# Sharing vector work by a port, placing small transposes, and unsplit products for eight more tiles in a fused attention and feed-forward kernel

## The chip, the cores and the metric

The kernel runs on one NeuronCore of one Trainium2 chip. The metric is device time of one execution in microseconds (us), as a median of several. The engines are named as in the profile: PE (TensorE, the matrix engine; PEld is its loading of the stationary operand), DVE (VectorE), ACT (ScalarE), POOL (GpSimd) and SP (SyncE, which here issues nearly all DMAs).

## The reference

Local attention with a few global tokens, followed by a maxout feed-forward layer over all 4352 tokens. Shortened:

```
# 8 batches, 8 heads, 512 local and 32 global tokens, head dimension 64, all float32
s_g  = scale * q_g @ [k_g, k_l]^T ; out_g = softmax(s_g) @ [v_g, v_l]
s_l  = scale * [q_l @ k_g^T, mask(q_l @ k_l^T, |i - j| <= 32)]
out_l = softmax(s_l) @ [v_g, v_l]
x = concat(out_g, out_l) laid out as (4352 tokens, 512)
h = max(max(x @ w1, x @ w2), x @ w3)          # w1, w2, w3: 512 x 768
out = h @ w_out                               # 768 x 512
```

The weights come in as 64-bit numbers and are made into float32 in the kernel.

## The kernel before, in words

**Tiles.** A tile is 128 query rows of two heads: 128 tiles in all, four (t = 0 to 3) for each pair of heads p, sixteen for each batch. The order is SEQ: tiles 0, 1, 4, 5, ... of the first batch, then in number order from 16 on. `i` counts places in SEQ; from 16 on, i and the tile's number are the same.

**Products.** [...] A split product writes a number as a float32r high part plus a float32r rest and adds two or three products; it needs vector work to make the parts (`copy` makes the high part, line 99; `sub` the rest, line 92). An unsplit product takes the float32 numbers as they are. Scores of tiles in NATK (0 to 19 before) and products with the values of tiles below NAT (20 before) are unsplit; for the others `split_q`, `split_k`, `split_v` and the second halves of `trans`, `transg` and `pv` do the splitting. The feed-forward layer is split throughout.

**One pass of the loop (line 548) for tile i.** `trans(i+1)` puts four transposes of the next tile's probabilities on PE (lines 345 and 346, into the one PSUM tile T) and moves them out; `scores(i+3)` (line 297) makes scores on PE, masks and takes the minimum of the negated scores on DVE (L325), exponentiates on ACT (L327), scales by the inverse sum with `times` (L111, L113 or L115, whichever engine gets it), and a DMA on SP's queue then writes them as float32r into `prob`; `pv(i)` (line 374) multiplies the transposed probabilities with the values. Once for each four tiles, `glob` and `glob_soft` do the same for the global queries, and `glob_soft` issues six DMAs into `probg`. `transg` (line 357) transposes one 128x128 piece of `probg` (L364) and puts its columns into the same tile `pt` that `pv` reads. In the kernel before, `transg` of tile i+1 stands late in pass i, three feed-forward products after `pv(i)`.

**Feed-forward work as filling.** `fill(n)` puts n feed-forward products (L424 layer one, L445 layer two) on PE between these steps: 21 a pass for i < 32, 18 after. Batch 0 is done from i = 8 on with 256-wide products in layer one, the others 512 wide. The weights (24 pieces) are turned into float32 by `convert` (lines 154 to 172) in the passes up to i = 23: four operations on DVE over SBUF data (L161, L162, L165, L166), a `copy` and a `sub` for each piece.

**Who does the vector work.** `least` (line 82) holds a planned load for DVE, ACT and POOL and gives each `copy`, `sub` and `times` to the engine with the lowest planned load after it; the costs are formulas in the width n. `settle(4500)` (line 87) keeps an engine that was idle from being far behind in the plan.

```
load = {"a": 0.0, "d": 0.0, "p": 0.0}
e = min(costs, key=lambda e: load[e] + costs[e]); load[e] += costs[e]
```

The tile framework places the recorded instructions of the engines and adds the waits; each engine then runs its own list in order, and so does each DMA queue.

Of the kernel before, what the change touches and what calls it, by code (L numbers as in the profile page):

```python
# [20 lines left out]
NP = H // 2  # L21
# [1 line left out]
KW = 576  # L23
NEG = -8.0e9

NATK = range(0, 20)
HIMAX = float(np.array(0x47EFFFFF, np.int32).view(np.float32))


# [25 lines left out]
def body(ctx, tc, kin, qin, vin, min_, win, out):  # L55
# [12 lines left out]
    small = ctx.enter_context(tc.tile_pool(name="small", bufs=2))  # L68


    load = {"a": 0.0, "d": 0.0, "p": 0.0}

    def width(ap):
        n = 1
        for x in ap.shape[1:]:
            n *= x
        return n

    def spend(e, ns):
        load[e] += ns  # L80

    def least(costs):
        e = min(costs, key=lambda e: load[e] + costs[e])
        load[e] += costs[e]
        return e

    def settle(ns):
        top = max(load.values()) - ns
        for e in load:
            load[e] = max(load[e], top)  # L90

    def sub(out, a, b, psum=False):
        n = width(out)
        c = {"d": n * 1.04 + (160 if psum else 110)}
        if not psum:
            c["p"] = n * 2.32 + 130
        (dve if least(c) == "d" else pool).tensor_tensor(out=out, in0=a, in1=b, op=ALU.subtract)  # L97

    def copy(out, a, psum=False):
        n = width(out)  # L100
        c = {"d": n * (1.04 if psum else 0.52) + (160 if psum else 150), "a": n * 0.833 + (150 if psum else 190)}
        if least(c) == "d":
            dve.tensor_copy(out=out, in_=a)
        else:
            act.copy(out=out, in_=a)  # L105

    def times(out, a, col):
        n = width(out)
        e = least({"d": n * 0.52 + 125, "a": n * 0.833 + 185, "p": n * 1.27 + 150})
        if e == "d":  # L110
            dve.tensor_scalar(out=out, in0=a, scalar1=col, scalar2=None, op0=ALU.mult)  # L111
        elif e == "a":
            act.activation(out=out, in_=a, func=AF.Copy, scale=col)  # L113
        else:
            pool.tensor_scalar(out=out, in0=a, scalar1=col, scalar2=1.0, op0=ALU.mult, op1=ALU.mult)  # L115
# [38 lines left out]
    def convert(n):  # L154
        r = raw[n].bitcast(I32).rearrange("p (n t) -> p n t", t=2)
        if n < 18:
            c = spare[n // 2 % 2 if n < 15 else 1][:, n % 2]
# [6 lines left out]
        yield  # L164
        dve.scalar_tensor_tensor(out=c, in0=r[:, :, 1], scalar=-0x40000000, in1=c, op0=ALU.bitwise_and, op1=ALU.bitwise_or)  # L165
        dve.scalar_tensor_tensor(out=c, in0=r[:, :, 0], scalar=29, in1=c, op0=ALU.logical_shift_right, op1=ALU.bitwise_or)  # L166
        spend("d", 1900)
        yield
        wt[n] = const.tile([128, 1024], F32R, name=f"w{n}", tag=f"w{n}")
        copy(weight(n, 0), f32(c))  # L170
# [18 lines left out]


    NS = 4 * B * NP
    NAT = 20
    EARLY = 16
    SEQ = [4 * p + t for h in range(2) for p in range(NP) for t in (2 * h, 2 * h + 1)] + list(range(16, NS))
    kraw, kst, qraw, qs, vraw, vs, xr, sc, pg, pts = [{} for _ in range(10)]
# [320 lines left out]
    def tile_at(i):  # L516
        return SEQ[i] if i < NS else NS
# [30 lines left out]
    for i, sl in enumerate(SEQ):  # L548
        p, t = divmod(sl, 4)
        b = p // NP  # L550
        settle(4500)
        if i % 16 == 0 and b > 1:
            fill(400)
            mm[0] = moe_local(b - 1)
        trans(tile_at(i + 1))
        first = i < 32
        fill(6 if first else 4)
        next_scores(i + 3)
        if i < 16:
            if i == 7:  # L560
                clear()
            if i in (10, 12):
                load_k((i - 2) // 2)
            if i == 14:
                split_k(5)
                load_k(6)
        elif t == 3:
            split_k(p + 2)
            load_k(p + 3)
        fill(5 if first else 4)  # L570
        pv(sl)
# [3 lines left out]
            elif t == 2 or i == 14:  # L575
                glob_soft(p + 1 if i >= 16 else 4)
        fill(3)
        if i + 1 >= EARLY:
            transg(tile_at(i + 1))
        fill(7)  # L580
        split_v(tile_at(i + 2))
        if i < 12:
# [82 lines left out]
```

## Time and profile before

| | |
|---|---|
| median of 3 runs | 860.33 us (859.11 to 861.3) |
| the profiled execution | 859.92 us |
| its span, first to last instruction | 858.0 us |
| PE busy | 813.2 us, 95% of the span |
| DVE, ACT, POOL busy | 631.0, 505.8, 526.4 us |
| mean granted TensorE clock | 0.990 |
| DMA | 98.72 MB, mean 115 GB/s |

Busy time of an engine counts an instruction from its start to its end, so an instruction that is held up while it runs counts as busy. PE's instructions overlap; the distance from one start to the next is their pace. "L12" is line 12 of the kernel before; in the changed kernel the same statements stand ten lines further down (L97 is L103, L115 is L125, L364 is L374, L424 is L434). The product with the values of tile 0 starts 11.8 us into the span, that of tile 16 at 93.6, of tile 20 at 121.3, of tile 24 at 145.0, of tile 28 at 164.4, of tile 127 at 735.5.

### The profile page before, as it was taken

The page shows a single profiled execution, that of the slowest core. Times are in us where ns is not written, and L with a number is a line of the kernel's source. Part 1 is how long each engine was busy: PE and PEld are TensorE (multiplying, and loading weights), DVE is VectorE, ACT ScalarE, POOL GpSimd, SP SyncE. Part 2 cuts the span into 40 slices and gives each one's busy share as a digit, 9 for nine tenths or more (in the row PEclk, how much of TensorE's full clock was granted, in tenths as well). Part 3 has the DMA queues.
Part 4 walks back from the last instruction along what each step waited for, and adds up shares of the span by engine and source line. Part 5 has one row for each costly group of instructions (what it writes and reads, how often), then busy time and mean ns, then how long its engine had stood idle before and what let it go on. Part 6 is the DMA issues. An engine that isn't in the chain of part 4 may idle for free.

```text
span 858.0 us, 16764 instructions
## 1 busy us (share of the span) xinstructions
PE 813.2 (95%) x4736; PEld 683.5 (80%) x4736; DVE 631.0 (74%) x2182; ACT 505.8 (59%) x1430; POOL 526.4 (61%) x695
## 2 busy tenths in 40 slices
PE   6877777999999999999999999999999999999997
PEld 5556667888888888888888888788888888777796
DVE  6999788978888887878787888787887876322111
ACT  6666566766675767676666666676667665212111
POOL 4779878766677667766776667666686656101211
PEclk9999799999999999999999999999999999999999
DMA  9843533353334333443325333433344332221000
GB/s 315 278 151 120 165 120 102 112 161 105 112 111 131 119 96 105 129 137 98 95 91 160 107 111 111 141 114 96 101 132 134 93 102 90 75 72 29 28 25 25
DMA packets 99580, 98.72 MB, mean 115 GB/s; under 512 B 21152, under 2 KB 87968, under 8 KB 99488
## 3 DMA queue, kind: packets, MB, share of 16 engines
q1 hardware_dynamic: 99344, 97.43, 36.5%
q8 instruction: 38, 0.62, 0.3%
q14 instruction: 54, 0.44, 0.2%
q10 hardware_dynamic: 144, 0.23, 0.1%
HBM read 60.39 MB, written 8.91 MB: 81 GB/s over the span
## 4 chain that ended last, share of the span: by engine, by line
PE 82%; DVE 5%; DMA 5%; POOL 4%; issue 2%; ACT 1%; SPq 0%; DVEq 0%; POOLq 0%; ACTq 0%
PE pm L424 47%; PE pm L445 16%; PE O L392 7%; PE S L322 5%; PE T L345 2%; DMA raw<-w_in 2%; PE T L346 2%; PE S L274 1%; POOL h L97 1%; DMA qn<-q_in 1%; POOL xs L97 1%; PE S L364 1%; POOL w L97 1%; POOL early L115 1%; DMA vraw<-v_in 1%
## 5 line engine op out<-in xcount | busy, mean ns | idle before, releaser
L424 PE MATMUL pm<-xs,w 128*128 128x512 f32 (+1 forms) x2160 | 501.5, 370 | 5.3 <-POOL w L97 3.8
L424 PEld LDWEIGHTS pm<-xs,w 128*128 128x128 f32 x2160 | 349.5, 191 | 56.2 <-POOL w L97 4.2
L445 PE MATMUL pm<-w,h 128*128 128x512 f32 x612 | 160.3, 399 | 1.8 <-POOL h L97 1.8
L97 POOL TENSOR_TENSOR qs<-qraw,qs 128x256 fp32r<-128x256 f32 x108 | 83.2, 770 | 75.6 <-issue 42.2
L97 POOL TENSOR_TENSOR h<-m,h 128x512 fp32r<-128x512 f32 (+1 forms) x60 | 72.3, 1205 | 87.8 <-ACT h L105 87.8
L445 PEld LDWEIGHTS pm<-w,h 128*128 128x128 f32 x612 | 107.2, 188 | 22.6 <-POOL h L97 3.7
L115 POOL TENSOR_SCALAR s<-s,z 128x224 f32<-128x224 f32 (+1 forms) x212 | 97.0, 467 | 42.8 <-ACT lox L105 18.5
L327 ACT ACTIVATE s<-s,nm 128x192 f32<-128x192 f32 (+1 forms) x224 | 103.3, 462 | 25.4 <-DVE nm L325 19.9
L433 DVE TENSOR_TENSOR m<-pm,m 128x512 f32<-128x512 f32 (+1 forms) x120 | 72.9, 607 | 49.4 <-PE pm L424 47.1
L97 DVE TENSOR_TENSOR pt<-T,pt 128x512 fp32r<-128x512 f32 x108 | 74.5, 690 | 38.8 <-ACT pt L105 36.4
L325 DVE CUSTOM_DVE_ANT_0 s<-S,mask 128x192 f32<-128x192 f32 (+1 forms) x224 | 74.6, 370 | 12.7 <-PE S L322 6.4
L97 POOL TENSOR_TENSOR vs<-vraw,vs 128x256 fp32r<-128x256 f32 x107 | 80.3, 751 | 4.9 <-ACT vs L105 4.0
L105 ACT CAST pt<-T 128x512 fp32r<-128x512 f32 x89 | 52.0, 584 | 46.9 <-PE T L346 46.8
L392 PE MATMUL O<-pt,vs 128*128 128x320 f32 (+1 forms) x432 | 77.8, 302 | 0.1
L392 PEld LDWEIGHTS O<-pt,vs 128*128 128x128 f32 x432 | 70.0, 189 | 9.3 <-DVE pt L97 0.3
L97 POOL TENSOR_TENSOR kst<-kraw,kst 64x576 fp32r<-64x576 f32 x48 | 70.6, 1471 | 5.6 <-DVE nm L325 1.5
L322 PEld LDWEIGHTS S<-kst,qs 128*128 128x128 f32 x432 | 64.4, 192 | 11.1 <-DVE nmg L278 3.2
L400 DVE TENSOR_TENSOR xr<-O,lox 64x160 f32<-64x160 f32 x216 | 67.9, 314 | 2.8
L105 ACT CAST qs<-qraw 128x256 fp32r<-128x256 f32 x90 | 36.6, 406 | 56.6 <-PE S L322 39.5
L322 PE MATMUL S<-kst,qs 128*128 128x192 f32 (+1 forms) x432 | 66.0, 275 | 1.2 <-DVE nmg L278 1.2
L398 DVE TENSOR_TENSOR lox<-O,lox 64x320 f32<-64x320 f32 x108 | 51.6, 478 | 13.4 <-ACT lox L105 7.2
L105 ACT CAST h<-m 128x512 fp32r<-128x512 f32 (+1 forms) x59 | 32.9, 558 | 40.6 <-DVE m L433 40.5
(118 smaller groups left out, 1196.4 us busy)
## 6 DMA issues: line engine op xcount, KB each, us to landing
vraw<-v_in SPq DMA_DIRECT2D x132, 128.0 KB, 2.3
qraw<-q_in SPq DMA_DIRECT2D x108, 128.0 KB, 2.2
prob<-s SPq DMA_DIRECT2D x56, 224.0 KB, 2.4
raw<-w_in SPq DMA_DIRECT2D x24, 512.0 KB, 4.8
prob<-s SPq DMA_DIRECT2D x56, 192.0 KB, 2.3
kraw<-k_in SPq DMA_DIRECT2D x27, 320.0 KB, 3.2
out_dram<-o SPq DMA_DIRECT2D x32, 256.0 KB, 2.3
qn<-q_in SPq DMA_DIRECT2D x21, 128.0 KB, 3.8
```

What stands on the lines that cost most here:

```text
L97: (dve if least(c) == "d" else pool).tensor_tensor(out=out, in0=a, in1=b, op=ALU.subtract)
L105: act.copy(out=out, in_=a)
L115: pool.tensor_scalar(out=out, in0=a, scalar1=col, scalar2=1.0, op0=ALU.mult, op1=ALU.mult)
L322: pe.matmul(ph[j][:, 0:n], lhsT=qs[sl][:, a, 128 * j:128 * j + 128], rhs=kst[p][:, j, c0:c0 + n], start=(a == 0), stop=(a == 1))
L325: dve.tensor_tensor_reduce(out=s[:, j, 0:n], in0=ph[j][:, 0:n], in1=mask[:, (1, 0, 1, 0)[t], 32 * (t == 0):32 * (t == 0) + n], scale=-0.12 ...
L327: act.activation(out=s[:, j, 0:n], in_=s[:, j, 0:n], func=AF.Exp, bias=nm[:, j:j + 1], scale=-1.0, accum_out=z[:, j:j + 1])
L392: pe.matmul(o[:, j, 0:320].rearrange("p (a q) -> p a q", a=2)[:, :, 0:n], lhsT=vs[sl][:, 2 * j + c].rearrange("p a d -> p (a d)"), rhs=pt[ ...
L398: dve.tensor_tensor(out=lo, in0=o[0:64, :, 160:320], in1=lo, op=ALU.add)
L400: dve.tensor_tensor(out=xr[p][64 * j:64 * j + 64, t], in0=o[0:64, j, 0:160], in1=lo[:, j], op=ALU.add)
L424: pe.matmul(ps[:, 0:n], lhsT=weight(3 * f + i, w)[:, 128 * k:128 * k + 128], rhs=xs[k][:, a, c0:c0 + n], start=(q == 0), stop=(q == 11))
L433: dve.tensor_tensor(out=m[:, 0:n], in0=ps[:, 0:n], in1=m[:, 0:n], op=ALU.max)
L445: pe.matmul(ps, lhsT=hh[f][:, a, 128 * t:128 * t + 128], rhs=weight(18 + f, w), start=(q == 0), stop=(q == 17))
```

## The change

Four things change.

1. **The sharing rule.** [...] While `shared` is true (i < 26) a DVE operation over SBUF data or a POOL operation adds its cost to its engine and to x, and counts as free when both are; the fixed parts of the costs are lower. From i = 26 on the rule is the old one but for some nanoseconds in the fixed parts.
2. **Unsplit products for more tiles.** NATK goes from 20 to 28 tiles (scores; tiles 20 to 27), NAT from 20 to 26 (values; tiles 20 to 25).
3. **The global transposes.** `transg(i)` now stands at the start of pass i, directly before `trans(i+1)`, and no longer ahead of the last seven products of pass i-1.
4. **Loads of keys.** With pair 5 unsplit, `split_k(5)` at i = 14 falls away, and `load_k(6)` moves from i = 14 to i = 19.

```
-NATK = range(0, 20)
+NATK = range(0, 28)
...
-    NAT = 20
+    NAT = 26
...
+    load = {"a": 0.0, "d": 0.0, "p": 0.0, "x": 0.0}
+    shared = [True]
...
     def least(costs):
-        e = min(costs, key=lambda e: load[e] + costs[e])
-        load[e] += costs[e]
-        return e
+        if not shared[0]:
+            costs = {es[0]: ns for es, ns in costs.items()}
+        es = min(costs, key=lambda es: max(load[e] for e in es) + costs[es])
+        spend(es, costs[es])
+        return es[0]
...
     def sub(out, a, b, psum=False):
-        n = width(out)
-        c = {"d": n * 1.04 + (160 if psum else 110)}
+        n, k = width(out), 0 if shared[0] else 45
+        c = {"d" if psum else "dx": n * 1.04 + 75 + k + (40 if k and psum else 0)}
         if not psum:
-            c["p"] = n * 2.32 + 130
+            c["px"] = n * 2.32 + 80 + k
...
     def times(out, a, col):
-        e = least({"d": n * 0.52 + 125, "a": n * 0.833 + 185, "p": n * 1.27 + 150})
+        e = least({"dx": n * 0.52 + 60 + 65 * k, "a": n * 0.833 + 190, "px": n * 1.27 + 170 - 20 * k})
...
         settle(4500)
+        shared[0] = i < 26
...
+        if i >= EARLY:
+            transg(sl)
         trans(tile_at(i + 1))
...
-            if i == 14:
-                split_k(5)
-                load_k(6)
         elif t == 3:
             split_k(p + 2)
+            if p == NP:
+                load_k(6)
             load_k(p + 3)
...
         fill(3)
-        if i + 1 >= EARLY:
-            transg(tile_at(i + 1))
         fill(7)
```

`copy` gets costs of the same kind ("dx" where it reads SBUF, "d" where it reads PSUM).

What this makes of the engines' lists is seen at three places. First PE, in the passes of the third batch: L364 (L374 after) is the global transpose, L345 and L346 (L355, L356) the four local ones, L424 (L434) the feed-forward products. Before:

```order
L424 MATMUL pm<-xs,w_1080 128x512 x3
L364 MATMUL S<-identr,probg_95 128x128
L424 MATMUL pm<-xs,w_1080 128x512
L424 MATMUL pm<-xs,w_1150 128x512 x6
L345 MATMUL T<-identr,prob_93 128x128
L346 MATMUL T<-identr,prob_93 64x128
L345 MATMUL T<-identr,prob_93 128x128
L346 MATMUL T<-identr,prob_93 64x128
L424 MATMUL pm<-xs,w_1150 128x512 x4
```

After, a place of the same kind:

```order
L434 MATMUL pm<-xs,w_901 128x512 x4
L434 MATMUL pm<-xs,w_976 128x512 x6
L374 MATMUL S<-identr,probg_95 128x128
L355 MATMUL T<-identr,prob_93 128x128
L356 MATMUL T<-identr,prob_93 96x128
L355 MATMUL T<-identr,prob_93 128x128
L356 MATMUL T<-identr,prob_93 96x128
L434 MATMUL pm<-xs,w_976 128x512 x4
```

The three and seven products on both sides of the global transpose are ten in a row now, and the five transposes follow each other. Second POOL, while pieces 9 to 12 of the weights are made (w_747 to w_901). Before:

```order
L97 TENSOR_TENSOR w_747<-spare,w_747 128x512
L97 TENSOR_TENSOR xs<-xr,xs 128x256
L115 TENSOR_SCALAR early<-early,z 128x192
L97 TENSOR_TENSOR w_757<-spare,w_757 128x512
L97 TENSOR_TENSOR w_826<-spare,w_826 128x512
L97 TENSOR_TENSOR h_666<-m,h_666 128x256
L115 TENSOR_SCALAR early<-early,z 128x224 x2
L97 TENSOR_TENSOR w_901<-spare,w_901 128x512
```

After:

```order
L103 TENSOR_TENSOR w_747<-spare,w_747 128x512
L103 TENSOR_TENSOR xs<-xr,xs 128x256
L103 TENSOR_TENSOR h_666<-m,h_666 128x256
L103 TENSOR_TENSOR w_901<-spare,w_901 128x512
L103 TENSOR_TENSOR xs<-xr,xs 128x256
```

The scaling of the softmax (early<-early,z) has left POOL for ACT, and two of the four subtractions for weights have gone to DVE. Counted over the lists up to the product with the values of tile 16, POOL has 17 subtractions for weights before and 8 after, 30 scalings of `early` before and 9 after, 6 of `s` before and none after, 8 subtractions for `xs` before and 3 after, and the 2 large subtractions for keys (kst, 64x576) are gone; DVE gets 9 subtractions for weights and 4 for `xs` that it did not have, ACT 25 scalings. Between the products with the values of tiles 16 and 28 DVE loses 12 additions xr<-O,lox, 6 lox<-O,lox, 6 subtractions pt<-T,pt and 7 pt<-S,pt. Third SP's queue around the load of the keys of pair 6 (kraw_1027 before):

```order
L334 DMA prob0_93<-s_930 128x2x192
L235 DMA qraw_1018<-q_in 128x256
L212 DMA kraw_1027<-k_in 128x640
L334 DMA prob1_94<-s_1002 128x2x224
L250 DMA vraw_1068<-v_in 128x256
```

After, it is kn_1424:

```order
L344 DMA prob0_93<-s_1094 128x2x224
L160 DMA raw22_1147<-w_in 128x512
L260 DMA vraw_1136<-v_in 128x256
L222 DMA kn_1424<-k_in 128x640
L245 DMA qn_1184<-q_in 128x256
```

It moved from between the probabilities of tiles 16 and 17 to behind those of tile 18.

More of the change, by code (lines that the diff above doesn't have):

```diff
@@ L68, in body @@
     small = ctx.enter_context(tc.tile_pool(name="small", bufs=2))
-    load = {"a": 0.0, "d": 0.0, "p": 0.0}
+    load = {"a": 0.0, "d": 0.0, "p": 0.0, "x": 0.0}
+    shared = [True]
     def width(ap):
@@ L77, in width, with spend @@
         return n
-    def spend(e, ns):
-        load[e] += ns
+    def spend(es, ns):
+        for e in es:
+            load[e] += ns
     def least(costs):
-        e = min(costs, key=lambda e: load[e] + costs[e])
-        load[e] += costs[e]
-        return e
+        if not shared[0]:
[3 more added lines that the diff above has]
+        return es[0]
     def settle(ns):
@@ L92, in sub @@
     def sub(out, a, b, psum=False):
-        n = width(out)
-        c = {"d": n * 1.04 + (160 if psum else 110)}
+        n, k = width(out), 0 if shared[0] else 45
+        c = {"d" if psum else "dx": n * 1.04 + 75 + k + (40 if k and psum else 0)}
         if not psum:
-            c["p"] = n * 2.32 + 130
+            c["px"] = n * 2.32 + 80 + k
         (dve if least(c) == "d" else pool).tensor_tensor(out=out, in0=a, in1=b, op=ALU.subtract)
     def copy(out, a, psum=False):
-        n = width(out)
-        c = {"d": n * (1.04 if psum else 0.52) + (160 if psum else 150), "a": n * 0.833 + (150 if psum else 190)}
+        n, k = width(out), 0 if shared[0] else 75
+        c = {"a": n * 0.833 + (80 if psum else 110) + k}
+        if psum:
+            c["d"] = n * 1.04 + 80 + k
+        else:
+            c["dx"] = n * 0.52 + 75 + k
         if least(c) == "d":
@@ L107, in times @@
     def times(out, a, col):
-        n = width(out)
-        e = least({"d": n * 0.52 + 125, "a": n * 0.833 + 185, "p": n * 1.27 + 150})
+        n, k = width(out), 0 if shared[0] else 1
+        e = least({"dx": n * 0.52 + 60 + 65 * k, "a": n * 0.833 + 190, "px": n * 1.27 + 170 - 20 * k})
         if e == "d":
@@ L166, in convert @@
         dve.scalar_tensor_tensor(out=c, in0=r[:, :, 0], scalar=29, in1=c, op0=ALU.logical_shift_right, op1=ALU.bitwise_or)
-        spend("d", 1900)
+        spend("dx", 1900)
         yield
```

## The prediction

> **What bounds the kernel now.** I read the stretches first, cut where the products with the values of tiles 0, 16, 20, 24, 28 and 32 start, then what PE waits for, then single rows. Columns: stretch, its length, busy time (instructions) of PE, PEld, DVE, ACT and POOL, PE's clock, DMA share, GB/s.
>
> ```profile
> 11.80:38.10 26.30, 22.78 (x156) 15.60 (x154) 26.21 (x85) 18.34 (x54) 20.62 (x24) 1.00 0.94 323
> 38.10:93.60 55.50, 42.23 (x301) 35.73 (x300) 51.68 (x141) 34.42 (x94) 45.13 (x45) 0.94 0.45 146
> 93.60:121.30 27.70, 19.59 (x144) 17.45 (x144) 23.44 (x73) 16.76 (x48) 21.84 (x25) 0.87 0.51 160
> 121.30:145.00 23.70, 18.05 (x143) 16.69 (x141) 21.38 (x75) 17.19 (x51) 18.34 (x26) 1.00 0.30 89
> 145.00:164.40 19.40, 18.41 (x141) 18.00 (x142) 16.64 (x69) 14.91 (x45) 14.85 (x23) 0.91 0.43 127
> 189.40:735.50 546.10, 544.33 (x3022) 458.67 (x3021) 440.66 (x1572) 361.80 (x1033) 366.36 (x502) 1.00 0.37 112
> ```
>
> There are two regimes. From 189 us on PE is busy 544.33 of 546.10 us: only PE's own list counts there. Up to tile 16 (two rows, 81.8 us) DVE is busy 77.9 us, 95%, and PE 65.0. In between (three rows, 70.8 us) PE is busy 56.1 and DVE 61.5: neither is full, and PE waits for chains. PE's waits before 160 us, in us, times, longest:
>
> ```profile
> PE T L345 <- POOL early L115: 10.1, 10, 1.6
> PE T L345 <- DMA prob<-s: 6.4, 3, 4.7
> PE pm L424 <- POOL w L97: 3.8, 2, 3.6
> PE S L364 <- DMA probg<-sg: 3.0, 1, 3.0
> ```
>
> POOL's scaling, POOL's weights and DMAs that follow POOL's scaling are what PE waits for. But DVE's 95% is partly not work. Its four weight operations up to tile 16 (mean ns of one at the end of the first part), and the same operations in single rows:
>
> ```profile
> L165 DVE SCALAR_TENSOR_TENSOR spare<-raw,spare 128x512 int32<-128x512 int32 x18 | 20.2, 1123 | 0.0
> L166 DVE SCALAR_TENSOR_TENSOR spare<-raw,spare 128x512 int32<-128x512 int32 x18 | 16.8, 936 | 0.0
> L162 DVE TENSOR_SCALAR spare<-spare 128x512 int32<-128x512 int32 x18 | 11.2, 628 | 0.0
> L161 DVE TENSOR_SCALAR spare<-spare 128x512 f32<-128x512 f32 x18 | 10.7, 599 | 0.2 <-ACT spare L160 0.2
> ...
> 18.09 1.80 DVE L165 SCALAR_TENSOR_TENSOR spare<-raw,spare 128x512 int32<-128x512 int32 x1
> 19.93 0.68 DVE L166 SCALAR_TENSOR_TENSOR spare<-raw,spare 128x512 int32<-128x512 int32 x1
> 25.08 0.40 DVE L162 TENSOR_SCALAR spare<-spare 128x512 int32<-128x512 int32 x1
> ```
>
> ```profile
> 18.05 1.28 POOL L97 TENSOR_TENSOR w<-spare,w 128x512 fp32r<-128x512 f32 x1 [0.36 <-DVE w L103]
> ```
>
> The DVE operation at 18.09 started just after one on POOL and ended 0.56 us after POOL's end: it stood still meanwhile. With 0.68 us as the free time of L165 and L166 and 0.40 of L161 and L162, standing still costs 18 x (0.443 + 0.256 + 0.228 + 0.199) = 20.3 us of these 81.8.
>
> **A. Up to tile 16: less on POOL, more on DVE and ACT.** What POOL did there:
>
> ```profile
> L97 POOL TENSOR_TENSOR w<-spare,w 128x512 fp32r<-128x512 f32 x17 | 23.7, 1396 | 5.4 <-ACT w L105 4.1 <-DVE w L103 1.2
> L115 POOL TENSOR_SCALAR early<-early,z 128x192 f32<-128x192 f32 x14 | 10.4, 750 | 2.3 <-DVE z L330 1.2 <-PE S L318 1.1
> L115 POOL TENSOR_SCALAR early<-early,z 128x224 f32<-128x224 f32 x14 | 9.8, 709 | 3.7 <-DVE z L331 1.5 <-DVE z L330 1.4 <-PE S L318 0.8
> L97 POOL TENSOR_TENSOR xs<-xr,xs 128x256 fp32r<-128x256 f32 x8 | 7.6, 944 | 3.0 <-DMA probg<-sg 1.6 <-ACT xs L105 1.4
> L115 POOL TENSOR_SCALAR s<-s,z 128x224 f32<-128x224 f32 x4 | 3.8, 950 | 0.1
> ```
>
> By the counts of the two lists POOL loses 9 x 1.396 + 21 x 0.73 + 5 x 0.944 + 6 x 0.95 = 38.3 us of its 65.8, 58%, not counting the keys. I let the standing still shrink with it: 0.58 x 20.3 = 11.8 us off DVE. DVE gains 9 subtractions for weights, priced at the 0.68 of L166 (also two SBUF inputs, 512 wide), and 4 for xs at about 0.4 (half as wide): 7.7 us. Net -4.1; with the 4.7 us wait for `prob`, behind POOL's queue and partly DVE's idle time, a little shorter, I take A = -5. The ends: +4 if DVE's new work is not paid back (half of it, since DVE has 3.9 us idle), and -16 if all 20.3 go and 4 of the new work hide. ACT is the cover: its 25 new scalings cost by this row 11.5 us, so it goes from 52.8 to about 64 of 77 us.
>
> ```profile
> 9.47 0.46 ACT L113 ACTIVATE early<-early,z 128x192 f32<-128x192 f32 x1 [0.37 <-DVE z L330]
> ```
>
> [...]
>
> **B. Tiles 16 to 28.** Of 70.8 us PE is busy 56.1; 10.2 of these lie in three stretches at half clock (the first and the last of the three),
>
> ```profile
> 100.60:104.00 3.40, 3.40 (x21) 2.73 (x20) 1.92 (x8) 1.51 (x5) 2.90 (x4) 0.50 0.29 82
> ...
> 144.90:148.40 3.50, 3.48 (x16) 3.48 (x16) 2.54 (x12) 3.01 (x9) 3.35 (x3) 0.51 0.59 177
> ```
>
> so at full clock PE would need 51.0. To this come the unsplit products. A score unsplit (first three rows) and split (last three), each with five filling products behind it:
>
> ```profile
> 73.86 0.92 PE L318 MATMUL S<-kn,qn 128*128 128x224 f32 x4
> 74.46 0.91 PE L424 MATMUL pm<-xs,w 128*128 128x256 f32 x5
> 75.30 0.66 PE L384 MATMUL O<-pt,vn 128*64 128x128 f32 x8
> ...
> 111.35 0.60 PE L322 MATMUL S<-kst,qs 128*128 128x224 f32 x4
> 111.79 0.76 PE L424 MATMUL pm<-xs,w 128*128 128x256 f32 x5
> 112.49 0.76 PE L384 MATMUL O<-pt,vraw 128*64 128x160 f32 x8
> ```
>
> From start to the third row 1.44 against 1.14 us: +0.30 for each of 8 tiles, 2.4 us. For values I see only the busy times (0.76 here for eight records, about the 0.7 of a split one), so +0.1 for 6 tiles, and about 1 us for the global scores of two pairs: +4, PE's floor is 55. All waiting gone would give -15.8. What ends the waiting: `split_q`, `split_k` and `split_v` of these tiles go from POOL and ACT, and DVE loses, by rows as below and the table of the list, some 12 us of its 61.5 (12 additions, 6 + 6 + 7 subtractions at 0.3 to 0.7 each), so no engine is over 80% in a stretch of 60 us. In the steady part DVE at 81% leaves PE full; here chains through DMAs stay. I take 60%: B = -9.5, ends -4 and -15.
>
> After the idle spells the clock fell to half, here after waits of 3.6 and 3.0 us. [...]
>
> **C. The rest: the transposes in a row.** PE is full, so its pace decides.
>
> ```profile
> 409.66 0.40 PE L424 MATMUL pm<-xs,w 128*128 128x512 f32 x1
> 409.89 0.22 PE L364 MATMUL S<-identr,probg 128*128 128x128 f32 x1
> 409.95 0.45 PE L424 MATMUL pm<-xs,w 128*128 128x512 f32 x1
> ...
> 410.24 0.61 PE L424 MATMUL pm<-xs,w 128*128 128x512 f32 x2
> ```
>
> A product takes 0.23 us to the next start, a transpose 0.06, but the product behind a transpose 0.29: 0.06 us that the four local transposes pay as well, once for all four. In a row the global one pays it no more: -0.06 for each of the 100 tiles from 28 to 127, C = -6 (ends -2, if part of it comes back between transposes, and -7).
>
> What this could lay open: the columns of the global transpose must be in `pt` before `pv`. Before, they had seven products more.
>
> ```profile
> 411.20 0.29 DVE L97 TENSOR_TENSOR pt<-S,pt 128x128 fp32r<-128x128 f32 x1
> 412.05 0.69 DVE L103 CAST pt<-T 128x512 fp32r<-128x512 f32 x1 [0.55 <-PE T L346]
> ```
>
> ```profile
> 411.60 0.22 PE L345 MATMUL T<-identr,prob 128*128 128x128 f32 x1
> 414.21 0.74 PE L392 MATMUL O<-pt,vs 128*128 128x320 f32 x4
> ```
>
> They were done 1.6 us after the transpose (409.89 to 411.49); now 2.6 us are left (411.60 to 414.21). It fits, with 1.0 us to spare, at no cost.
>
> **D. The keys of pair 6** are loaded one to two tiles before `glob` needs them, in SP's queue behind DMAs that wait for a softmax: once 0 to +3 us, taken as +1. The rule from i = 26 on is the old one within nanoseconds; what it hands over between DVE and ACT (some 20 copies) lies beside a full PE: 0.
>
> **The sum.** 859.92 - 5 - 9.5 - 6 + 1 = 840.4 us, against the profiled execution's own time, 0.4 below the median of 860.33. I say 840.
>
> **Rivals.** *All of the vector waiting goes* (A -16, B -12, C -6, D +1): 827. For it: PE's busy time of 65.0 in A is far under 81.8. Against: DVE's own work there is still some 65 us. 0.18.
> *The early gain is eaten by ACT and DVE's new work* (A 0, B -4): 859.92 - 4 - 6 + 1 = 851. For it: ACT goes to 84% in A and stands in each tile's softmax, and the sharing may hold up other operations than the ones I counted. Against: POOL's row is the one that PE waited for most. 0.16.
> *Slower: the global columns come late.* If the copy and the subtraction behind the transpose take 1.3 us longer than in the row above, since ACT and DVE are at that moment busy with the end of the pass, `pv` waits 0.3 us in each of 100 tiles, +30 in place of -6; with A and B as taken, 876. It decides from 1.0 us on. Against: DVE is idle 0.55 us before it takes the next local transposes (the row at 412.05), so its list is empty there. 0.05.
> *The plan changes little*: since only a plan decides who works, new collisions may cost what old ones did, with all four terms near 0, within 0.3%: 0.03.
>
> **Numbers.** My forecast has 0.58. A difference of 0.3%, 2.6 us, is about what can be told from none. Forecast and the first two rivals are all faster: 0.92; same 0.03; slower 0.05. The range reaches down to 825, to take in the first rival, and up to 852 for the second.
>
> **What the profile after would show.** A right: DVE's L175 and L176 (L165, L166 before) at a mean under 0.85 us, POOL under half busy up to tile 16, and tile 16 about 5 us earlier. B right: tile 28 near 150 us, fewer half-clock stretches. C right: in the steady part a period of 4 tiles shorter by 0.24 us, no wait of L402 for pt. D: a wait of L280 for the key load at tile 20. I am wrong if tile 16 comes no earlier, or if PE in the last 500 us waits for DVE or ACT.

## The result, and the profile after

The changed kernel takes 834.75 us (median of 4, 834.39 to 838.82); the kernel before, on the same chip, 860.63 us (median of 4, 859.11 to 861.3). The ratio is 0.9712, with an interval of 0.968 to 0.9745: 2.9% faster. The forecast of 840 was 5 us too high; the measured time lies inside its range, 825 to 852. The span fell by 25.4 us, from 858.0 to 832.6. Cut at the starts of the products with the values, as before:

| stretch | before | after | measured | forecast |
|---|---|---|---|---|
| up to tile 0 | 11.8 | 12.2 | +0.4 | 0 |
| tile 0 to 16 (A) | 81.8 | 71.4 | -10.4 | -5 |
| tile 16 to 28 (B, and D) | 70.8 | 59.8 | -11.0 | -9.5 + 1 |
| tile 28 to 127 (C) | 571.1 | 567.3 | -3.8 | -6 |
| behind tile 127 | 122.4 | 121.9 | -0.5 | 0 |

The same stretches of the kernel after (columns as in the prediction: stretch, length, busy time of PE, PEld, DVE, ACT and POOL, clock, DMA share, GB/s):

```profile
12.20:35.80 23.60, 20.86 (x154) 15.13 (x153) 23.03 (x84) 19.46 (x57) 9.60 (x12) 1.00 0.96 339
35.80:83.60 47.80, 42.96 (x311) 36.45 (x310) 46.36 (x149) 40.79 (x114) 13.26 (x13) 0.93 0.61 196
83.60:103.80 20.20, 18.67 (x150) 15.95 (x149) 18.97 (x69) 16.58 (x50) 7.43 (x6) 1.00 0.49 149
103.80:122.50 18.70, 18.18 (x148) 16.01 (x148) 16.55 (x63) 13.57 (x43) 5.52 (x6) 1.00 0.39 110
122.50:143.40 20.90, 19.06 (x150) 17.92 (x150) 16.60 (x66) 14.16 (x43) 13.65 (x20) 0.92 0.54 158
168.10:710.70 542.60, 539.98 (x3023) 460.62 (x3022) 442.99 (x1590) 363.68 (x1010) 368.87 (x506) 1.00 0.37 113
```

Up to tile 16 (two rows) DVE is still the full engine, 69.4 of 71.4 us, but with 8.5 us less on it; POOL fell from 65.8 to 22.9 us and ACT rose to 60.2, 84%. From 16 to 28 (three rows) PE, busy 55.9 of 59.8 us, is now the full one. In the steady part PE is as full as it was; its own list got shorter.

What PE waits for before 160 us, us in total, times, longest:

```profile
PE S L328 <- DMA qn<-q_in: 4.5, 1, 4.5
PE T L355 <- ACT early L123: 2.3, 5, 1.1
PE T L355 <- DMA prob<-s: 2.0, 3, 0.8
PE T L355 <- DVE z L341: 1.7, 1, 1.7
...
PE S L328 <- DVE nm L335: 1.4, 1, 1.4
PE T L355 <- POOL early L125: 0.8, 1, 0.8
PE T L355 <- ACT pt L115: 0.8, 1, 0.8
```

The wait for POOL's scaled tile is 0.8 us, was 10.1; that for ACT's is 2.3. The first row is the start of the kernel and was there before (4.5 us). No key load is in the whole list, and no product with the values (L394, L402) waits there for `pt`: the one row with `pt` is a transpose that waits until ACT has moved the tile before out of T. So neither the cost of D nor the slower rival came.

DVE's four weight operations up to tile 16, the subtractions that it took over, and what POOL kept of them:

```profile
L175 DVE SCALAR_TENSOR_TENSOR spare<-raw,spare 128x512 int32<-128x512 int32 x18 | 17.6, 977 | 0.0
L176 DVE SCALAR_TENSOR_TENSOR spare<-raw,spare 128x512 int32<-128x512 int32 x17 | 12.9, 756 | 0.0
L171 DVE TENSOR_SCALAR spare<-spare 128x512 f32<-128x512 f32 x17 | 9.4, 565 | 0.0
L172 DVE TENSOR_SCALAR spare<-spare 128x512 int32<-128x512 int32 x18 | 7.3, 413 | 0.0
L103 DVE TENSOR_TENSOR w<-spare,w 128x512 fp32r<-128x512 f32 x9 | 6.2, 691 | 0.7 <-ACT w L115 0.7
```

```profile
L103 POOL TENSOR_TENSOR w<-spare,w 128x512 fp32r<-128x512 f32 x8 | 10.8, 1345 | 26.4 <-ACT w L115 26.0 <-DVE w L113 0.4
```

The four means add up to 2.71 us for a weight, against 3.29 before and 2.16 by the free times of 0.68 and 0.40 (the shortest of L165, L166, L162 and L161 in that stretch of the kernel before took 676, 673, 396 and 401 ns). What is left of the standing still is 18 x (2.71 - 2.16) = 9.9 us of 20.3.

A tile's transposes in the steady part, the columns being start, length of the group, engine, line:

```profile
403.50 2.50 PE L434 MATMUL pm<-xs,w 128*128 128x512 f32 x10
405.83 0.22 PE L374 MATMUL S<-identr,probg 128*128 128x128 f32 x1
405.89 0.23 PE L355 MATMUL T<-identr,prob 128*128 128x128 f32 x1
405.96 0.23 PE L356 MATMUL T<-identr,prob 128*64 128x128 f32 x1
406.03 0.24 PE L355 MATMUL T<-identr,prob 128*128 128x128 f32 x1
406.11 0.22 PE L356 MATMUL T<-identr,prob 128*64 128x128 f32 x1
406.17 1.15 PE L434 MATMUL pm<-xs,w 128*128 128x512 f32 x4
```

Five in a row start 0.06, 0.07, 0.07 and 0.08 us apart: between local transposes it is a little more than the 0.06 that the prediction used.

### The profile page after: what moved, and what is told of

Its sections match the earlier page's. It is cut to its first block, busy times and chain, and to the rows that moved or that the text cites. A ratio compares the mean times of both kernels' runs of the same rounds, so it can differ in the third digit from the quotient of the medians.

```text
span 832.6 us, 16650 instructions
## 1 busy us (share of the span) xinstructions
PE 807.9 (97%) x4760; PEld 684.4 (82%) x4760; DVE 615.7 (74%) x2192; ACT 510.6 (61%) x1423; POOL 458.3 (55%) x618
## 4 chain that ended last, share of the span: by engine, by line
PE 79%; DVE 2%; POOL 1%; DMA 1%; issue 1%; ACT 0%; SPq 0%; POOLq 0%; DVEq 0%
PE pm L434 45%; PE pm L455 15%; PE O L402 6%; PE S L332 5%; PE T L355 2%; PE T L356 2%; PE S L284 1%; POOL h L103 1%; PE S L374 1%; PE O L510 1%; PE S L280 1%; POOL xs L103 0%; DMA prob<-s 0%; DVE s L335 0%; DVE kst L113 0%
## 5 line engine op out<-in xcount | busy, mean ns | idle before, releaser
L434 PE MATMUL pm<-xs,w 128*128 128x512 f32 (+1 forms) x2160 | 491.3, 367 | 1.1 <-ACT m L115 0.7
L434 PEld LDWEIGHTS pm<-xs,w 128*128 128x128 f32 x2160 | 353.2, 190 | 51.6 <-issue 4.5
L455 PEld LDWEIGHTS pm<-w,h 128*128 128x128 f32 x612 | 109.1, 188 | 22.5 <-POOL h L103 4.2
L103 POOL TENSOR_TENSOR qs<-qraw,qs 128x256 fp32r<-128x256 f32 x100 | 77.0, 770 | 67.6 <-issue 34.2
L443 DVE TENSOR_TENSOR m<-pm,m 128x512 f32<-128x512 f32 (+1 forms) x120 | 72.8, 607 | 55.1 <-PE pm L434 54.5
L125 POOL TENSOR_SCALAR s<-s,z 128x224 f32<-128x224 f32 (+1 forms) x193 | 84.9, 448 | 35.6 <-ACT lox L115 17.8
L103 DVE TENSOR_TENSOR pt<-T,pt 128x512 fp32r<-128x512 f32 x102 | 70.4, 690 | 20.5 <-ACT pt L115 19.4
L103 POOL TENSOR_TENSOR vs<-vraw,vs 128x256 fp32r<-128x256 f32 x102 | 76.1, 746 | 9.4 <-ACT vs L115 6.9
L402 PEld LDWEIGHTS O<-pt,vs 128*128 128x128 f32 x408 | 66.6, 189 | 8.7
L402 PE MATMUL O<-pt,vs 128*128 128x320 f32 (+1 forms) x408 | 73.2, 301 | 0.0
L115 ACT CAST pt<-T 128x512 fp32r<-128x512 f32 x102 | 60.3, 591 | 13.7 <-PE T L356 11.5
L332 PEld LDWEIGHTS S<-kst,qs 128*128 128x128 f32 x400 | 59.7, 191 | 9.2 <-DVE nmg L288 1.0
L410 DVE TENSOR_TENSOR xr<-O,lox 64x160 f32<-64x160 f32 x204 | 64.4, 316 | 3.2
L103 POOL TENSOR_TENSOR kst<-kraw,kst 64x576 fp32r<-64x576 f32 x43 | 62.7, 1457 | 5.8 <-ACT kst L115 1.7
L125 POOL TENSOR_SCALAR sg<-sg,zg 64x544 f32<-64x544 f32 x32 | 23.9, 746 | 71.1 <-ACT pt L115 33.2
L332 PE MATMUL S<-kst,qs 128*128 128x192 f32 (+1 forms) x400 | 60.1, 272 | 0.1
```

The costliest lines, as they stand in the source:

```text
L332: pe.matmul(ph[j][:, 0:n], lhsT=qs[sl][:, a, 128 * j:128 * j + 128], rhs=kst[p][:, j, c0:c0 + n], start=(a == 0), stop=(a == 1))
L402: pe.matmul(o[:, j, 0:320].rearrange("p (a q) -> p a q", a=2)[:, :, 0:n], lhsT=vs[sl][:, 2 * j + c].rearrange("p a d -> p (a d)"), rhs=pt[ ...
L410: dve.tensor_tensor(out=xr[p][64 * j:64 * j + 64, t], in0=o[0:64, j, 0:160], in1=lo[:, j], op=ALU.add)
L434: pe.matmul(ps[:, 0:n], lhsT=weight(3 * f + i, w)[:, 128 * k:128 * k + 128], rhs=xs[k][:, a, c0:c0 + n], start=(q == 0), stop=(q == 11))
L443: dve.tensor_tensor(out=m[:, 0:n], in0=ps[:, 0:n], in1=m[:, 0:n], op=ALU.max)
L455: pe.matmul(ps, lhsT=hh[f][:, a, 128 * t:128 * t + 128], rhs=weight(18 + f, w), start=(q == 0), stop=(q == 17))
```

## The experiments

The theory at this point: up to tile 16 the gain is DVE's standing still and PE's waits for POOL; from 16 to 28 it is splitting work that is gone; behind that it is one entry and exit of the row of transposes. The rivals were that one part makes all of it, or that the parts help each other. The stretches of all runs, and the median beside that of the kernel before on the same chip. The stretches come from one profiled execution of each run. Two pairs of runs have nearly the same lists up to tile 16 (the rule alone and the rule alone up to tile 16; the kernel after and the same with the rule up to tile 16) and differ there by 2.6 and 1.6 us, so a difference of that size in a stretch is not told from none:

| kernel | median | ratio (interval) | 0 to 16 | 16 to 28 | 28 to 127 |
|---|---|---|---|---|---|
| before | 859.5 to 859.9 | 1 | 81.8 | 70.8 | 571.1 |
| transposes in a row alone | 856.72 | 0.9966 (0.9955 to 0.9976) | 81.1 | 72.0 | 568.8 |
| unsplit products alone | 852.28 | 0.991 (0.9893 to 0.9927) | 78.1 | 64.4 | 573.7 |
| rule alone | 852.49 | 0.9921 (0.9905 to 0.9936) | 72.3 | 73.7 | 572.4 |
| all but the row | 839.2 | 0.9759 (0.9745 to 0.9772) | 71.0 | 60.6 | 572.0 |
| after, POOL reads added | 858.21 | 0.9983 (0.9972 to 0.9994) | 93.7 | 59.9 | 566.3 |
| after, POOL writes added | 846.27 | 0.9842 (0.9822 to 0.9861) | 82.3 | 61.0 | 567.4 |
| before, scaling on ACT | 865.12 | 1.0063 (1.0046 to 1.008) | 85.2 | 71.2 | 573.2 |
| before, transposes behind `pv` | 859.38 | 0.9996 (0.9987 to 1.0005) | 81.6 | 71.5 | 570.3 |
| after, weights on DVE | 837.93 | 0.9758 (0.9742 to 0.9775) | 71.1 | 60.8 | 567.6 |
| before, weights on DVE | 860.22 | 1.0009 (1.0 to 1.0018) | 78.7 | 72.1 | 572.8 |
| rule alone, up to tile 16 | 850.54 | 0.9903 (0.9888 to 0.9918) | 69.7 | 70.8 | 572.2 |
| after, rule up to tile 16 | 839.36 | 0.9768 (0.9751 to 0.9786) | 73.0 | 62.8 | 567.2 |

### The parts one by one

**Transposes in a row alone**, in the kernel before:

```
+        if i >= EARLY:
+            transg(sl)
         trans(tile_at(i + 1))
...
-        if i + 1 >= EARLY:
-            transg(tile_at(i + 1))
```

> The kernel before with the global transposes alone moved into the row. My theory: PE's pace alone pays, and the steady part gave 3.8 us over 100 tiles in the full change, so about -4 us here (856.6), -6 at most, and nothing before tile 16. Rival one: the 3.8 us come from the changed sharing plan (other hands for 20 copies) and not from the row; then this stays within 1 us of 860.6. Rival two: the row is worth the forecast 6 us and something else in the full change gave 2 us back; then -6.

Measured: 856.72, 3.0 us less than the 859.73 beside it. The part works alone and is worth half of the 6 us forecast.

**Unsplit products alone**:

```
-NATK = range(0, 20)
+NATK = range(0, 28)
...
-    NAT = 20
+    NAT = 26
...
-            if i == 14:
-                split_k(5)
-                load_k(6)
...
+            if p == NP:
+                load_k(6)
```

> The kernel before with the unsplit products of tiles 20 to 27 alone, old sharing rule, old place of the transposes. My theory: it pays only where those tiles are made, tiles 16 to 28, and there only part, since POOL still scales the softmax and stands in the chains: -5 to -8 us, tile 16 no more than 2 us earlier, so about 854. Rival: the unsplit products carry all of the 11 us between tiles 16 and 28, whatever the rule: -11 or more, 849.

Measured: 852.28, 7.5 us less. The stretch from 16 to 28 gains 6.4 us, not the 9.5 that the forecast gave to this part. The stretch up to tile 16 is 3.7 us shorter, where at most 2 had been expected, and that behind tile 28 is 2.6 us longer; why is open.

**The rule alone** (the new `load`, `least`, `sub`, `copy` and `times`, and `shared[0] = i < 26`):

> The kernel before with the sharing rule to tile 25 alone. My theory: the rule carries all of the 10 us up to tile 16, since nothing else of the change acts there but the missing split of one pair of keys, and some 3 to 5 us after it: -13 to -15, about 846, with the weight operations on DVE near the means of the full change (0.98 and 0.76 us). Rival: the gain needs the unsplit products too, since with split ones the work taken from POOL lands on a DVE that is full: -5 or less, 855.

Measured: 852.49, 7.2 us less, between the two. Up to tile 16 the rule has nearly all of A (-9.5), but from 16 to 28 it is 2.9 us *longer* in the profiled execution, where a gain of 3 to 5 had been expected. That expectation fell.

**All but the row** (the kernel after, with the global transposes back between the two groups of products):

> The full change with the global transposes back in their old place. If the three parts add up by place, it lacks the 3.8 us of the steady part: 834.8 + 4 = 839. If the row also helps in tiles 16 to 28, by looser timing of the DMA into probg, it lacks 6 or more: 841. If the steady gain came from the changed plan: within 1 us of 834.8.

Measured: 839.2, so the row is worth 4.5 us in the whole. The three parts alone give 3.0 + 7.5 + 7.2 = 17.7 us; the rule and the unsplit products together give 20.5, not 14.7. Some 6 us come only when both are there, and the table says where: from tile 16 to 28 the rule alone is +2.9, the unsplit products alone -6.4, both -10.2.

### Why the rule is worth more beside the unsplit products

**The rule alone, but only up to tile 16**:

```
-        shared[0] = i < 26
+        shared[0] = i < 16
```

> The run with the rule alone, with the new rule ending at tile 16 instead of 26; behind that the old costs. There the stretch from tile 16 to 28 took 73.7 us, 2.9 longer than in the kernel before. Theory (in that stretch the rule takes work from GpSimd and puts it on VectorE and ScalarE, which are also splitting keys, queries and values): the stretch is back at 70 to 71.5 us and the time is 849 to 850.5. Rival (the stretch inherits what the first 16 tiles did faster: PE's other work was pulled ahead or transfers come late): 73 to 74 us again, the time 852 to 853.

**The kernel after with the same edit**:

> The kernel after, with the new rule ending at tile 16 instead of 26. Its stretch from tile 16 to 28 took 59.8 us; with the unsplit products and the old rule it took 64.4. Theory (with the splitting gone VectorE and ScalarE have room, and there the rule's sharing gains what it loses beside the splitting): the stretch takes 63 to 65 us and the time is 838 to 840. Rival (the better stretch is inherited from an earlier start of it, and the rule matters only up to tile 16): 59 to 61 us and 834 to 836.

Measured: 850.54, at the upper end of the theory's range, and 839.36, inside it. The stretch from 16 to 28 takes 70.8 us, as the theory has it, and 62.8, just under its 63 to 65 and over the rival's 61. That stretch in four runs, the rule alone, then alone up to 16, then all up to 16, then the unsplit products with the old rule:

```profile
84.30:158.00 73.70, 58.39 (x428) 52.99 (x428) 61.01 (x222) 56.34 (x166) 39.30 (x47) 0.93 0.37 114
```

```profile
82.50:153.30 70.80, 58.38 (x429) 53.52 (x429) 65.21 (x220) 50.10 (x147) 59.03 (x74) 0.90 0.40 120
```

```profile
86.30:149.10 62.80, 54.70 (x442) 48.32 (x442) 48.58 (x188) 39.26 (x121) 44.10 (x56) 1.00 0.42 131
```

```profile
90.30:154.70 64.40, 57.06 (x448) 50.46 (x448) 50.12 (x184) 38.50 (x122) 47.13 (x58) 0.97 0.49 151
```

Compare the first two rows. The new rule takes 20 us off POOL there and puts 6 on ACT; DVE loses 4, some of which was standing still (L175 and L176 take 784 and 778 ns there, against 925 and 997 with the rule stopped). The stretch is longer all the same, and with the rule alone PE waits there for the subtraction on DVE that splits probabilities, which isn't among its waits in the kernel before:

```profile
PE O L402 <- DVE pt L103: 3.6, 5, 1.3
```

With the rule stopped at tile 16 the stretch is back at the 70.8 us of the kernel before, though it begins 11 us earlier, which speaks for a loss inside the stretch and not for one handed on from what went before. But this loss is near the spread: the medians of the two runs are 852.49 and 850.54, the intervals of their ratios overlap (0.9905 to 0.9936 and 0.9888 to 0.9918), and the profiled executions are the longest of four and the shortest of four. Where nothing is split (third and fourth row against the 59.8 of the kernel after) ACT has 39 us of work and DVE 49 of 63; there the rule has room to move POOL's work to, and gains 3.0 us. That it gains there is shown: 834.75 against 839.36, with intervals that lie apart (0.968 to 0.9745 and 0.9751 to 0.9786). That it is worth more there than beside the splitting is shown too, by the 20.5 us against 14.7 above. That it loses beside the splitting is likely and not shown, and that room is the reason is argued from the busy times.

### Which piece of the rule makes A

**Before, with the scaling of the first 16 tiles always on ACT**:

```
-            times(s[:, j, 0:n], s[:, j, 0:n], z[:, j:j + 1])
+            if sl < EARLY:
+                act.activation(out=s[:, j, 0:n], in_=s[:, j, 0:n], func=AF.Copy, scale=z[:, j:j + 1])
+                spend("a", n * 0.833 + 185)
+            else:
+                times(s[:, j, 0:n], s[:, j, 0:n], z[:, j:j + 1])
```

> The kernel before, with one decision changed: the scaling of the first 16 tiles' probabilities is always ScalarE's, where the old rule gave most of it to GpSimd. Theory (of the 10 us that the new rule gains up to tile 16, most come from GpSimd's result being waited for and its reads, and the scaling is the larger part): tile 16 comes 6 us earlier, at 87 to 88 instead of 93.6, PE's wait for GpSimd's scaled tile (10.1 us in the kernel before) is gone, and the time is 852 to 855. Rival (it is the weights' subtractions on GpSimd that cost): less than 2 us, the time 858 to 860.

**Before, with the weights' subtractions on DVE**:

```
-        sub(weight(n, 1), f32(c), f32(weight(n, 0)))
+        if n < 18:
+            dve.tensor_tensor(out=weight(n, 1), in0=f32(c), in1=f32(weight(n, 0)), op=ALU.subtract)
+            spend("d", 512 * 1.04 + 110)
+        else:
+            sub(weight(n, 1), f32(c), f32(weight(n, 0)))
```

> The kernel before, with the subtractions of the first 18 weights on VectorE and all else left to the old rule. VectorE gets 17 x 0.69 = 11.7 us more. Theory (in the run that moved GpSimd's scaling to ScalarE the four weight operations kept their sum of 3.2 us, so the 20 us of standing still belong to GpSimd's subtractions): the sum of the four means falls from 3.29 to 2.4 to 2.6 us, 12 to 16 us less, and PE's waits for GpSimd (10.1 us for the scaled tile) shrink: tile 16 4 to 8 us earlier, the time 852 to 856. Rival (the new work is not paid back): tile 16 3 to 6 us later, the time 863 to 866.

Both expectations missed on the time, and the first theory, that scaling is the larger piece, fell. Scaling on ACT was 5.3 us *slower*, the weights on DVE changed nothing (0.7 us more). The weight operations from 12.2 to 93.6 us bear on why each piece is not enough, first with the scaling on ACT, then with the weights on DVE:

```profile
L166 DVE SCALAR_TENSOR_TENSOR spare<-raw,spare 128x512 int32<-128x512 int32 x17 | 18.1, 1065 | 0.0
L161 DVE TENSOR_SCALAR spare<-spare 128x512 f32<-128x512 f32 x18 | 16.0, 895 | 2.3 <-ACT spare L160 2.3
L165 DVE SCALAR_TENSOR_TENSOR spare<-raw,spare 128x512 int32<-128x512 int32 x17 | 14.0, 825 | 0.0
L162 DVE TENSOR_SCALAR spare<-spare 128x512 int32<-128x512 int32 x18 | 7.9, 443 | 0.0
```

```profile
L172 DVE TENSOR_TENSOR w<-spare,w 128x512 fp32r<-128x512 f32 x18 | 14.6, 813 | 0.8 <-ACT w L105 0.8
L165 DVE SCALAR_TENSOR_TENSOR spare<-raw,spare 128x512 int32<-128x512 int32 x18 | 13.9, 771 | 0.0
L166 DVE SCALAR_TENSOR_TENSOR spare<-raw,spare 128x512 int32<-128x512 int32 x18 | 12.8, 709 | 0.0
L161 DVE TENSOR_SCALAR spare<-spare 128x512 f32<-128x512 f32 x17 | 10.6, 633 | 0.0
L162 DVE TENSOR_SCALAR spare<-spare 128x512 int32<-128x512 int32 x18 | 8.6, 475 | 0.0
```

With the scaling gone from POOL the four means still add up to 3.23 us: the standing still stays, and DVE is busy 81.8 of 85.2 us. Some 5 us of that are new work: the plan, with the scaling charged to ACT, gave DVE 5 casts of `w`, 7 copies of `xr` and 2 of `pt` that ACT had done (counted in the records of both traces). With the subtractions gone the four add up to 2.59, as expected, and the standing still falls to 18 x 0.43 = 7.7 us: most of it belonged to POOL's subtractions of weights. But that run keeps the other half, the wait for POOL's scaled tile. PE's largest wait for scaled tiles, first with the scaling on ACT, then with the weights on DVE:

```profile
PE T L349 <- ACT early L333: 5.6, 7, 1.8
```

```profile
PE T L349 <- POOL early L115: 9.6, 10, 1.9
```

One run takes away PE's wait for POOL, with 5.6 us for ACT in its place, and leaves DVE full; the other relieves DVE (72.8 of 78.7 us busy) and leaves PE's wait. Up to tile 16 they give +3.4 and -3.1 us; the rule, which does some of both, -9.5. This fits two limits that had to go together, but it is argued: no run has just these two pieces, and the copies that the plan moved to DVE may be what made the first run slower.

**After, with the weights on DVE** (the same edit in the kernel after, planned as `spend("dx", 512 * 1.04 + 75)`):

> The kernel after, with the weights' subtractions of the first 18 weights all on VectorE (nine of them were, eight were GpSimd's at 1.35 us each). VectorE gets 8 x 0.69 = 5.5 us more; GpSimd keeps 12 of its 22.9 us up to tile 16. Theory (VectorE stands still only for GpSimd's long subtractions): L175 and L176 (977 and 756 ns in the kernel after) come near 0.7 us each, the standing still falls from 9.7 to 2 to 4 us, which pays for the new work: tile 16 between 1 us later and 3 us earlier, the time 832 to 836. Rival (the standing still goes with all of GpSimd's work, scaling too): half of it stays, tile 16 comes 3 to 5 us later, the time 838 to 840.

Measured: 837.93. The stretch up to tile 16 is 71.1 us, 0.3 less, and L175 and L176 take 719 and 711 ns, as the theory has it; the four means add up to 2.43, which leaves 18 x 0.27 = 4.8 us of standing still, a little over the 2 to 4 expected. The median lies just under the rival's time. The profiled execution can't say why: at 835.55 us it is the shortest of the four, and the only one at full clock throughout. It isn't better than the kernel after, whose interval of the ratio it overlaps. No run of the study beat the kernel after.

### Work added to POOL

**Reads**, in the kernel after (and below, **writes**, with five `pool.memset(extra, 0.0)` in place of the two):

```
+    extra = const.tile([128, 512], F32, name="extra")
+    pool.memset(extra, 0.0)
...
+        for _ in range(2 if i < 16 else 0):
+            pool.tensor_tensor(out=extra, in0=extra, in1=extra, op=ALU.subtract)
```

> The kernel after, with two subtractions of 128x512 that nobody needs (a scratch tile minus itself) put on GpSimd in each of the first 16 passes: 32 of them, by the 1.3 us of such a subtraction about 41 us of GpSimd work that reads SBUF, which is what the new rule took from GpSimd up to tile 16. Theory (VectorE stands still while GpSimd reads): L175 and L176, at 977 and 756 ns in the kernel after, go back towards the 1.1 and 0.93 us of the kernel before; some 10 us of standing still return, tile 16 comes near 91 to 93 instead of 83.6 and the time is about 843. Rival (the gain came because chains no longer wait for a slow result of GpSimd): nobody waits for these subtractions, so L175 and L176 may lengthen but tile 16 moves by less than 3 us, and the time is 835 to 837.

> The kernel after, with five fills of a scratch tile of 128x512 on GpSimd, which read nothing, in each of the first 16 passes: about as long a GpSimd work as the two subtractions of the run beside it. Theory (VectorE stands still only for GpSimd's reads of SBUF): L175 and L176 stay within 0.1 us of 977 and 756 ns, tile 16 moves by 0 to 3 us, the time is 835 to 838. Rival (any GpSimd work holds VectorE): the same loss as in the run with subtractions, about 843. [...]

Measured: 858.21 with reads and 846.27 with writes, both over every expectation. The weight operations (two lines further down than in the kernel after: L173 is L171, L177 is L175) and DVE's subtraction for weights, with reads (12.7 to 106.4 us, up to tile 16) and with writes (12.2 to 93.6 us):

```profile
L177 DVE SCALAR_TENSOR_TENSOR spare<-raw,spare 128x512 int32<-128x512 int32 x18 | 17.6, 979 | 0.0
L178 DVE SCALAR_TENSOR_TENSOR spare<-raw,spare 128x512 int32<-128x512 int32 x17 | 15.5, 911 | 0.0
L173 DVE TENSOR_SCALAR spare<-spare 128x512 f32<-128x512 f32 x18 | 13.1, 739 | 0.0
L174 DVE TENSOR_SCALAR spare<-spare 128x512 int32<-128x512 int32 x18 | 10.7, 600 | 0.0
L103 DVE TENSOR_TENSOR w<-spare,w 128x512 fp32r<-128x512 f32 x9 | 7.7, 850 | 0.2 <-ACT w L115 0.2
```

```profile
L173 DVE TENSOR_SCALAR spare<-spare 128x512 f32<-128x512 f32 x18 | 14.1, 792 | 0.0
L178 DVE SCALAR_TENSOR_TENSOR spare<-raw,spare 128x512 int32<-128x512 int32 x17 | 13.9, 816 | 0.0
L177 DVE SCALAR_TENSOR_TENSOR spare<-raw,spare 128x512 int32<-128x512 int32 x18 | 13.8, 764 | 0.0
L174 DVE TENSOR_SCALAR spare<-spare 128x512 int32<-128x512 int32 x18 | 11.0, 615 | 0.0
L103 DVE TENSOR_TENSOR w<-spare,w 128x512 fp32r<-128x512 f32 x9 | 6.2, 685 | 0.0
```

With reads the four add up to 3.23 us, near the 3.29 of the kernel before: of the 10.4 us of standing still that had gone, 18 x 0.52 = 9.3 came back. But the stretch lost 22.3. "Nobody waits for them" was wrong: POOL was busy for 44.5 of the 46.6 us from 12.7 to 59.3, the added subtractions stood in its list ahead of its own results, and PE waited for these results. With reads:

```profile
PE T L357 <- POOL early L125: 8.5, 6, 5.6
```

It was 0.8 us. PE's clock was lower too. The stretch up to tile 16, with reads and with writes:

```profile
12.70:106.40 93.70, 70.82 (x460) 55.50 (x459) 82.98 (x235) 60.86 (x172) 57.46 (x57) 0.85 0.56 184
13.00:95.30 82.30, 68.61 (x460) 53.66 (x459) 76.24 (x236) 60.49 (x172) 65.58 (x103) 0.90 0.63 209
```

PE's mean clock is 0.85 and 0.90 there, against 0.95 in the kernel after. How much of the 22 us is the queue, how much the standing still and how much the clock, these two runs can't separate, and the run doesn't prove the theory by its time. Of how the engines meet they do tell something, below.

### The row of transposes

**Before, with the global transposes directly behind the product with the values**:

```
         pv(sl)
...
-        fill(3)
         if i + 1 >= EARLY:
             transg(tile_at(i + 1))
+        fill(3)
         fill(7)
```

> The kernel before, with the global transposes of the next tile issued directly behind the product with the values, ahead of the products of the experts that filled the gap, instead of between two such groups. They still enter and leave the row of products once each, as before. Theory (what the row saves is the one entry and exit of the transpose mode, about 4 us in the 111 tiles from 16 on): no change, within 1.3 us of the kernel before. Rival (it is the neighbour that decides, a product of the attention beside a transpose costing less than one of the experts): 3 to 4 us earlier, as with the transposes in one row (856.7).

Measured: 859.38, a ratio of 0.9996 (0.9987 to 1.0005). Another neighbour in front saves nothing that can be told, 0.4 us; only joining the row does, 3.0 us. This is what the theory of one entry and exit has, and the rival falls; that PE changes a mode there is not shown.

## Why the prediction was right or wrong, point by point

**Direction and order of size: right.** Faster was given 0.92, and apart from D's +1 every term had the right sign. That the total came out 5 us too high is the balance of one term far too small, one near and one too big.

**A: the mechanism held in part, the size didn't (-5, measured -10.4).** The standing still shrank by 10.4 us where 11.8 had been taken, and DVE's new work was 6.2 + 1.6 us where 7.7 had been taken. (The prediction priced the subtraction on DVE at L166's 0.68 us; the subtraction itself took 0.691.) The sign "L175 and L176 under 0.85 us" failed for L175 (977 ns); POOL, at 22.9 of 71.4 us, is under half as forecast. The step that failed is the net of -4.1 on DVE, to which only "a little" was added for PE's waits. DVE's busy time fell by 8.5 us, of which the two amounts above make 2.6. It lost some small operations and their own standing still as well: one of 64x1 (L286) took 1.26 us in the kernel before and 0.15 after, and a 1.04 us cast of `h` is gone from the list. Two weight operations fewer are counted in the stretch (17 of L171 and L176), 1.3 us; the rest isn't accounted for. And PE's 10.1 us of waits for POOL's scaled tile, which the prediction quoted and then left out of A, shrank to 0.8. That both had to go is argued from the two experiments on pieces of the rule: DVE relieved alone gives 3.1 us, the scaling moved alone loses 3.4 (with copies moved to DVE), and the rule, which eases both, gives 9.5. The second rival gave this stretch 0, since ACT would stand in each tile's chain. ACT did go to the 84% that it said, and PE waits 2.3 us for it. It cost far less than what went.

**B: the size was nearly right (-9.5, measured -11.0), for a reason that was half missing.** The prediction gave it to the splitting work alone. That work alone is worth 6.4 us; taking 60% of the waiting as gone was too much. The other 4 or so come from the new rule inside the stretch, which the prediction never priced there, and which pays there since the splitting is gone (-3.0 to -3.8; beside the splitting +2.9 in the one profiled execution, near the spread). Tile 28 was to come near 150 us and came at 143.4; half-clock stretches were to become fewer and went from four to two in the first 160 us. No run shows the -12 that the first rival takes for this stretch; the kernel after took 11.0 us less there.

**C: the mechanism held, the term was somewhat too big (-6, measured -3.8).** The loss of one entry and exit is real: 3.0 us alone, 4.5 in the whole. Over all runs the stretch from 28 to 127 takes 566.3 to 568.8 us in the six with the row and 570.3 to 573.7 in the eight without; the means are 567.4 and 572.2, so 4.8 us is a fairer size than the 3.8 of one pair. What was mis-sized is named in the prediction's own lower end: part comes back between the transposes. From start to start, averaged over 520 us of the steady part (some 90 tiles; worked out from the records of both traces), a transpose of L345 was followed by the next 0.064 us later before and 0.074 after, and the global one by its successor 0.059 before and 0.069 after. Summed over what follows every transpose but a tile's last local one, this is 22.5 us before and 25.7 after, so some 3 us were given back. The product behind the global transpose took 0.283 us to the next start before, one behind a product 0.231, so 0.052 us a tile were saved and not 0.06. These two alone would leave some 2 us; where the rest of the gain comes from is open, and why transposes in a longer row start further apart wasn't tried. Four tiles of this stretch took 23.07 us before and 22.92 after, shorter by 0.15 where 0.24 was forecast.

**D: no cost (+1, measured none).** No wait for a key load is in PE's list. The slower rival didn't come either: no product with the values waits for `pt`.

## What to carry to other kernels

When a stretch has a full engine and, beside it, another engine's results that the matrix engine waits for, price both: here a piece of the rule that went for one of them alone gave 3 us or a loss, and the rule, which eased both, 9.5. The worth of a rule that spreads work depends on what else is on the engines: the rule and the unsplit products together gave some 6 us more than the two runs alone add up to, so measure the parts of a change together as well as alone. And work that nobody reads isn't free if a later result on the same engine is waited for: put on POOL it took the time from 834.75 to 858.21 us (reads) and 846.27 (writes) here, and PE's wait for POOL's scaled tile from 0.8 to 8.5 and 2.0 us.

## What the runs showed of the hardware

**Which operations of DVE meet POOL's.** POOL's fills, which read nothing, lengthened the two TENSOR_SCALAR forms (565 to 792 ns and 413 to 615), which have one tensor as input, and left those with two tensors at 1.58 us for the pair, against 1.73 in the kernel after. POOL's subtractions lengthened TENSOR_SCALAR nearly as much (739 and 600) and, of the forms with two tensors, L176 (756 to 911) and DVE's subtraction for weights (691 to 850; 685 with the fills), but not L175 (977 and 979). So TENSOR_SCALAR took longer beside POOL's reads and beside its fills, and DVE's subtraction for weights beside the reads alone; L175 didn't with either. What the two engines meet at, no run shows: the port of the title, and the load x that the plan keeps for it, are the author's assumption.

**Float32 and float32r on PE.** In the kernel before, the transposes of `early`, which is float32, start 0.11 us apart (L345 and L346 at 72.70, 72.81, 72.92 and 73.03 us), those of `prob`, which is float32r, 0.06 to 0.07 (105.55, 105.61, 105.67 and 105.74).

**The clock falls without a full idle spell.** In the kernel after, the two half-clock stretches were 6.8 and 3.4 us long. The two stretches ahead of them, and then the slow ones:

```profile
38.10:41.10 3.00, 0.92 (x9) 0.68 (x10) 3.00 (x9) 2.80 (x7) 0.21 (x1) 1.00 0.74 261
133.00:136.70 3.70, 1.98 (x19) 1.83 (x18) 3.29 (x15) 2.32 (x8) 2.46 (x5) 0.99 0.74 219
```

```profile
41.10:47.90 6.80, 5.66 (x21) 4.56 (x21) 6.80 (x23) 5.73 (x17) 2.69 (x2) 0.50 0.01 2
136.70:140.10 3.40, 3.40 (x17) 3.40 (x16) 2.81 (x12) 2.35 (x8) 2.28 (x5) 0.50 0.24 69
```

PE was busy 0.92 of 3.0 and 1.98 of 3.7 us there, with no single wait over 1.7 us. The prediction had taken waits of 3.0 and 3.6 us for the cause; in this trace half clock came behind stretches in which PE was busy for 31 and 54% of the time. Several short waits, the longest of 1.7 us, were followed by as much half clock (3.4 us from 136.7 on) as the one wait of 3.6 us in the kernel before (3.4 us from 100.6 on). Over all fourteen traces (worked out from their records) the clock changes lie on a grid of 3.41 us. Of the pieces of this grid at full clock, in the first 700 us, 46 were followed by half clock: PE was busy for 0 to 53% of 44 of them, and for 59 and 64% of the other two. Of the 2714 that were followed by full clock, all but two had PE busy for over 50%, and the least busy of all for 49%. In the kernels before and after alone it was 0 to 50% for the six followed by half clock and 54% or more for the other 390. So what goes with the fall in these traces is PE's busy share of such a piece, and not one wait of a given length.
